# A new prologue and a split last tile in a kernel of windowed attention and a gated feed-forward layer

## Chip, core and metric

The kernel runs on one core of a Trainium2 chip. The metric is the device time of one execution in microseconds (us). Times are medians of several executions, and the profile is one more execution under the hardware profiler; its span is about 1.7 us shorter than the time.

The profile names the engines PE (matmul), PEld (weight load), DVE (vector), ACT (scalar), POOL and SP (which here only issues DMAs).

## The reference

Causal attention over a window of 64 positions, for 8 batches, 8 heads, 576 positions and head size 64, feeds a SwiGLU layer over 4608 tokens (512 to 1536 to 512).

```python
scores = (1/8) * q @ k.T                       # per batch and head
mask = (rel >= 0) & (rel < 64)                 # rel = query position - key position
attn = softmax(where(mask, scores, -1e9))
x = (attn @ v), heads side by side             # 4608 x 512
out = (silu(x @ w_gate) * (x @ w_val)) @ w_out # float32
```

## The kernel before

All engines get their instructions from one list; a helper derives the semaphore waits from what each operation reads and writes. Each engine works through its own part in program order. An operation that waits holds up all that is behind it on its engine.

A tile is 128 tokens. For tile n, `T(n)` transposes q and k, `Sx(n, half)` makes the scores of four heads and the exponential, `AV(n, half)` multiplies by v and normalizes, and `X(n)` transposes the result into xT for the feed-forward part. `F(c, f)` makes one of 12 blocks of the hidden layer (hT) for a chunk of four tiles, and `O(c, u)` the output of one tile. The loaded tiles are kn, qn and va, and T leaves its results in kT and qz. F(0,0) begins with the first matmul on Wg, so "the first Wg matmul" below marks the end of the prologue. The first four tiles have their own prologue, because the first F needs all four.

```python
def first_T(self, pr):                    # one head pair: k and q share a PSUM bank
    tb = bank[:, :].bitcast(BF).rearrange("p (w j t) -> p w j t", w=2, j=4)
    # PE: 8 transposes; then DVE copies k to kT, ACT and DVE copy the halves of q to qz
    g.op("act", ... qz half 0 ..., reads=[bk, (bk, "k")])   # after the k copy
    g.op("dve", ... qz half 1 ..., reads=[bk])

def init_nmask(self):                     # additive mask, made from the 0/1 mask
    self.g.op("dve", lambda e: e.tensor_scalar(self.nmask[:, :], m[:, :], -1.0, 30000.0, ALU.add, ALU.mult), ...)

def load_v(self, n):                      # va: v of tile n.  vb: v shifted by 64 rows, made from va by DMA
    ... pool: va <- v in HBM
    g.op("sp", lambda e: e.dma_start(vb[64:128], va[0:64]), reads=lo, ...)
    g.op("sp", lambda e: e.dma_start(vb2[0:64], va[64:128]), reads=hi, ...)   # vb of tile n + 1

# build(), prologue
self.first_casts(0); self.init_pt(); self.first_T(0); self.first_T(1)
self.first_casts(1); self.init_nmask()
self.Sx(0, 0, True); self.Sx(1, 0, True)
self.first_T(2); self.Sx(2, 0, True)
self.first_T(3); self.Sx(3, 0, True)
for n in range(4):
    self.Sx(n, 1, True); self.AV(n, 0)
for n in range(4):
    self.AV(n, 1)
    if n > 0: self.X(n - 1, "act")
self.X(3, "act")
... # then F(0, 0..5), T(4), F(0, 6), ...

# build(), end: the last chunk's F, with O of the chunk before between them, then
for u in range(4):
    self.O(NFC - 1, u)        # 12 matmuls of 512 columns, one ACT copy, one DMA from SP
```

The softmax here doesn't subtract the row's maximum and nothing guards it: scores larger than these inputs give would overflow.

## Time and profile before

| kernel before | |
|---|---|
| time, median | 376.6 us |
| span of the profile | 375.07 us |
| PE busy | 352.3 us (94%) |
| end of the last xT copy, after which F(0,0) starts | 25.83 us |
| last stretch of idle PE that ends on hT | 361.24 us |

The first lines are from the page: the span, the busy times, the busy tenths of PE in 40 slices and the engines' shares in the chain of waits.

```profile
span 375.1 us, 6635 instructions
PE 352.3 (94%) x2624; PEld 192.0 (51%) x2624; DVE 254.6 (68%) x550; ACT 152.3 (41%) x260; POOL 107.5 (29%) x136
PE   1589999999899999999999999999999999999986
PE 81%; DVE 13%; ACT 3%; DMA 2%; issue 1%
```

PE is full except in the first two or three slices (9.4 us each) and a little at the end. A change of prologue and end can only win what is there. The next lines are PE's timeline in the prologue (start, duration, engine, line, operation; in brackets the idle time before it and what ended it).

```profile
7.68 1.89 PE L302 MATMUL ps<-ident,c 128*128 128x128 bf16 x16 [7.68 <-ACT c L292]
12.69 0.29 PE L388 MATMUL ps<-nmask,ident 128*128 128x128 bf16 x1 [3.12 <-DVE nmask L266]
12.77 0.32 PE L389 MATMUL ps<-qz,kT 128*128 128x128 bf16 x1
12.88 0.32 PE L388 MATMUL ps<-nmask,ident 128*128 128x128 bf16 x1
...
18.65 0.23 PE L388 MATMUL ps<-nmask,ident 128*128 128x128 bf16 x1 [0.72 <-DVE qz L317]
18.71 0.22 PE L389 MATMUL ps<-qz,kT 128*128 128x128 bf16 x1
18.77 0.22 PE L388 MATMUL ps<-nmask,ident 128*128 128x128 bf16 x1
...
21.18 0.19 PE L419 MATMUL ps<-vb,pt 128*128 128x65 bf16 x1
...
25.88 1.04 PE L466 MATMUL ps<-xT,Wg 128*128 128x512 bf16 x4 [0.69 <-ACT xT L450]
```

PE waits 3.12 us for the mask bias (nmask) and later for a copy on DVE (qz). AV(3), at 21.18 us, waits for nothing: the last vb copy that it needs had landed at 19.42. Look at the starts, too: near 12.8 us the matmuls start every 0.107 us, near 18.7 us every 0.056 us. PE's clock has doubled in between. The trace's clock record, which starts with the switch, puts it at 17.73 us.

The end, from the timeline of all engines:

```profile
360.50 0.69 DVE L476 SCALAR_TENSOR_TENSOR hT<-uu,ps 128x512 bf16<-128x512 bf16 x1
361.24 10.54 PE L489 MATMUL ps<-Wo,hT 128*128 128x512 bf16 x48 [1.27 <-DVE hT L476]
...
371.81 0.60 ACT L494 ACTIVATE ost<-ps 128x512 f32<-128x512 f32 x1 [1.99 <-PE ps L489]
372.43 0.33 SPq L496 DMA_DIRECT2D out_dram<-ost  x1
```

PE idles for the elementwise work of the last F, then makes the last four output tiles. Behind the last of them stand an ACT copy of 0.60 us and a DMA of 256 KB.

### The profile page before, as it was taken

The page shows a single profiled execution, that of the slowest core. Times are in us where ns is not written, and L with a number is a line of the kernel's source. Part 1 is how long each engine was busy: PE and PEld are TensorE (multiplying, and loading weights), DVE is VectorE, ACT ScalarE, POOL GpSimd, SP SyncE. Part 2 cuts the span into 40 slices and gives each one's busy share as a digit, 9 for nine tenths or more (in the row PEclk, how much of TensorE's full clock was granted, in tenths as well). Part 3 has the DMA queues.
Part 4 walks back from the last instruction along what each step waited for, and adds up shares of the span by engine and source line. Part 5 has one row for each costly group of instructions (what it writes and reads, how often), then busy time and mean ns, then how long its engine had stood idle before and what let it go on. Part 6 is the DMA issues. An engine that isn't in the chain of part 4 may idle for free.

```text
span 375.1 us, 6635 instructions
## 1 busy us (share of the span) xinstructions
PE 352.3 (94%) x2624; PEld 192.0 (51%) x2624; DVE 254.6 (68%) x550; ACT 152.3 (41%) x260; POOL 107.5 (29%) x136
## 2 busy tenths in 40 slices
PE   1589999999899999999999999999999999999986
PEld 1564555555455555555555555555555555444432
DVE  6668876688867777777777777777777777655520
ACT  2553535435444444444444444444444444233311
POOL 8985525434222222322222222422220000000000
PEclk9999999999999999999999999999999999999999
DMA  9999999979957777777888787877771000010012
GB/s 236 202 201 175 204 173 205 169 47 91 84 71 85 86 86 87 82 88 87 90 87 89 78 94 86 86 83 77 78 82 37 30 29 30 28 58 28 28 38 104
DMA packets 126158, 35.61 MB, mean 95 GB/s; under 512 B 108272, under 2 KB 121520, under 8 KB 126128
## 3 DMA queue, kind: packets, MB, share of 16 engines
q0 software_dynamic: 113152, 17.83, 64.3%
q1 hardware_dynamic: 11920, 16.31, 13.5%
q10 hardware_dynamic: 1056, 1.05, 0.9%
q8 instruction: 21, 0.34, 0.4%
q14 instruction: 9, 0.07, 0.1%
HBM read 37.75 MB, written 9.44 MB: 126 GB/s over the span
## 4 chain that ended last, share of the span: by engine, by line
PE 81%; DVE 13%; ACT 3%; DMA 2%; issue 1%
PE ps L466 41%; PE ps L489 25%; PE ps L389 5%; DVE hT L476 4%; DVE uu L474 4%; PE ps L360 3%; PE ps L441 2%; PE ps L420 2%; PE ps L419 2%; DVE xb L429 2%; DMA f<-in_q_dram 2%; ACT sig L472 1%; DVE pt L407 1%; ACT qz L366 1%; PE ps L302 1%
## 5 line engine op out<-in xcount | busy, mean ns | idle before, releaser
L474 DVE SCALAR_TENSOR_TENSOR uu<-sig,ps 128x512 bf16<-128x512 bf16 x108 | 74.1, 686 | 65.1 <-ACT sig L472 65.1
L466 PE MATMUL ps<-xT,Wg 128*128 128x512 bf16 x432 | 111.0, 380 | 2.4 <-DVE xT L448 1.7
L466 PE MATMUL ps<-xT,Wv 128*128 128x512 bf16 x432 | 110.9, 379 | 0.0
L489 PE MATMUL ps<-Wo,hT 128*128 128x512 bf16 x432 | 98.7, 380 | 2.1 <-DVE hT L476 2.1
L472 ACT ACTIVATE sig<-ps 128x512 bf16<-128x512 f32 x108 | 64.0, 592 | 43.4 <-PE ps L466 43.4
L277 POOL DMA_DIRECT2D qn<-in_q_dram x36 | 30.4, 847 | 164.2 <-PE ps L360 161.3
L476 DVE SCALAR_TENSOR_TENSOR hT<-uu,ps 128x512 bf16<-128x512 bf16 x108 | 74.2, 687 | 3.7
L466 PEld LDWEIGHTS ps<-xT,Wv 128*128 128x128 bf16 x432 | 42.2, 98 | 51.0
L489 PEld LDWEIGHTS ps<-Wo,hT 128*128 128x128 bf16 x432 | 40.9, 98 | 46.9 <-DVE hT L476 2.7
L401 ACT ACTIVATE pt<-ps 128x512 bf16<-128x512 f32 x72 | 42.9, 596 | 33.2 <-PE ps L389 30.5
L466 PEld LDWEIGHTS ps<-xT,Wg 128*128 128x128 bf16 x432 | 38.2, 98 | 32.6 <-DVE xT L448 2.0
L494 ACT ACTIVATE ost<-ps 128x512 f32<-128x512 f32 x36 | 21.5, 597 | 74.8 <-PE ps L489 74.8
L366 ACT ACTIVATE qz<-ps 64x512 bf16<-64x512 bf16 x32 | 18.9, 590 | 57.8 <-DVE kT L365 57.8
L328 POOL DMA_DIRECT2D va<-in_v_dram x40 | 34.7, 875 | 1.3 <-DVE wup L226 0.8
L389 PE MATMUL ps<-qz,kT 128*128 128x128 bf16 x288 | 30.8, 225 | 2.0 <-ACT qz L366 0.4
L429 DVE TENSOR_TENSOR xb<-ps,rc 128x256 bf16<-128x256 f32 x72 | 30.6, 425 | 2.5
L277 POOL DMA_DIRECT2D kn<-in_k_dram x36 | 30.7, 858 | 1.2 <-DMA Wv<-in_moe_w_val_dram 0.8
L448 DVE COPY xT<-ps 128x512 bf16<-128x512 bf16 x32 | 13.6, 423 | 24.1 <-PE ps L441 24.1
L407 DVE TENSOR_TENSOR pt<-pt,mask 128x512 bf16<-128x512 bf16 x64 | 26.6, 416 | 1.5 <-ACT pt L401 1.4
L419 PE MATMUL ps<-vb,pt 128*128 128x65 bf16 x288 | 26.9, 194 | 0.1
L420 PE MATMUL ps<-va,pt 128*128 128x65 bf16 x288 | 27.0, 194 | 0.0
L419 PEld LDWEIGHTS ps<-vb,pt 128*128 128x128 bf16 x288 | 22.6, 98 | 7.3 <-DVE xT L448 0.2
(44 smaller groups left out, 198.6 us busy)
## 6 DMA issues: line engine op xcount, KB each, us to landing
out_dram<-ost SPq DMA_DIRECT2D x36, 256.0 KB, 2.0
vb<-va SPq DMA_DIRECT2D x71, 80.0 KB, 2.1
va<-in_v_dram POOLq DMA_DIRECT2D x32, 128.0 KB, 4.5
qn<-in_q_dram POOLq DMA_DIRECT2D x28, 128.0 KB, 3.4
kn<-in_k_dram POOLq DMA_DIRECT2D x28, 128.0 KB, 4.4
Wo<-in_moe_w_out_dram POOLq DMA_DIRECT2D x2, 768.0 KB, 19.2
Wg<-in_moe_w_gate_dram POOLq DMA_DIRECT2D x5, 256.0 KB, 12.7
Wv<-in_moe_w_val_dram POOLq DMA_DIRECT2D x5, 256.0 KB, 13.3
```

The costliest lines, as they stand in the source:

```text
L277: self.g.op("pool", lambda e, d=d, a=a: e.dma_start(d, a), writes=ks, dma=True)
L328: g.op("pool", lambda e, d=d, a=a: e.dma_start(d, a), writes=ks, dma=True)
L389: r = e.matmul(sv[:, w, c], self.kT[:, pr, k0:k0 + 128], qz[:, pr, :, 64 * w:64 * w + 64], start=not bias, stop=True)
L401: g.op("act", lambda e: e.activation(po, si, ACTF.Exp, scale=SCALE), reads=[bk], writes=[pk])
L419: e.matmul(av[:, j, :], pt[:, h, 0:128], vb[:, h, 0:65], start=True, stop=False)
L420: r = e.matmul(av[:, j, :], pt[:, h, 64:192], va[:, h, 0:65], start=False, stop=True)
L429: g.op("dve", lambda e: e.tensor_tensor(xo, av[:, :, 0:64], rb, ALU.mult), reads=[bk, ("rc", ir)], writes=[("xb", ix, half)])
L466: r = e.matmul(bank[:, :], W[:, kk, f * 128:f * 128 + 128], xT[:, kk, :], start=(kk == 0), stop=(kk == NK - 1))
L472: g.op("act", lambda e: e.activation(sig[:, :], G[:, :], ACTF.Tanh, scale=0.5), reads=[gk], writes=[("sig", i)])
L474: g.op("dve", lambda e: e.scalar_tensor_tensor(uu[:, :], sig[:, :], 1.0, G[:, :], ALU.add, ALU.mult), reads=[("sig", i), gk], writes=[("uu ...
L476: g.op("dve", lambda e: e.scalar_tensor_tensor(hT[:, f, :], uu[:, :], 0.5, V[:, :], ALU.mult, ALU.mult), reads=[("uu", i), vk], writes=[(" ...
L489: r = e.matmul(OB[:, :], hT[:, f, 128 * u:128 * u + 128], self.Wo[:, f, :], start=(f == 0), stop=(f == NF - 1))
```

## The change

The intent is to shorten both ends. In the prologue, k and q are transposed into separate PSUM banks with larger copies, nmask is built on POOL with no detour over mask, and 13 dummy matmuls on zeros run while PE waits for data, to bring up its clock. At the end, O of the tile before goes behind the last F, and the last tile is made as two column halves, copied by two engines and stored from two queues.

```diff
+        g.op("dve", lambda e: e.memset(self.wz[:, :], 0.0), writes=["wz"])
+        g.op("dve", lambda e: e.memset(self.nmask[:, :], 0.0), writes=["nmask"])
-    def init_pool_b(self):          # mask only, then init_nmask on DVE
+    def init_mask(self, m, key, fill):   # the same three POOL operations for nmask and for mask
...
-    def first_T(self, pr):
+    def first_T(self, which, half):      # two head pairs of k, or of q, in one bank
...
+            g.op("dve", lambda e: e.tensor_copy(kd, ks), reads=[bk], writes=kk)   # 128x1024
...
+    def warm(self, count):
+                r = e.matmul(bank[:, :], self.wz[:, 0:128], self.wz[:, :], start=True, stop=True)
...
+    def O_last(self, c, u):              # two halves of 256 columns: ACT + SP queue, DVE + ACT queue
...
-        self.first_casts(0)
+        self.warm(13)
         self.init_pt()
-        (first_T(0), first_T(1), first_casts(1), init_nmask, Sx and first_T(2), first_T(3) interleaved)
+        for half in range(2):
+            self.first_cast("k", half)
+            self.first_cast("q", half)
+        for half in range(2):
+            self.first_T("k", half)
+            self.first_T("q", half)
+        for n in range(4):
+            self.Sx(n, 0, True)
...
+                late = c == NFC - 1 and u == 3
-                if c > 1:
+                if c > 1 and not late:
                     self.O(c - 1, u)
                 self.F(c, 3 * u + 2)
+                if late:
+                    self.O(c - 1, u)
...
-        for u in range(4):
+        for u in range(3):
             self.O(NFC - 1, u)
+        self.O_last(NFC - 1, 3)
```

More of the change, by code (lines that the diff above doesn't have):

```diff
@@ L190, in alloc @@
         self.nmask = sb("nmask", 4 * 64)
+        self.wz = sb("wz", 512)
         self.pt = [t[:, :].rearrange("p (h x) -> p h x", h=H) for t in ring("pt", self.NP, H * 192)]
@@ L251, in init_pool_a @@
             pattern=[[-1, 128]], channel_multiplier=1), writes=["ident"])
-    def init_pool_b(self):
-        m = self.mask
+    def init_mask(self, m, key, fill):
         mm = m[:, :].rearrange("p (a q) -> p a q", a=4)
         self.g.op("pool", lambda e: e.affine_select(
-            out=mm, in_=mm, compare_op=ALU.is_gt, fill=0.0, base=0,
-            pattern=[[0, 4], [-1, 64]], channel_multiplier=1), writes=["mask"])
+            out=mm, in_=mm, compare_op=ALU.is_gt, fill=fill, base=0,
+            pattern=[[0, 4], [-1, 64]], channel_multiplier=1), writes=[key])
         self.g.op("pool", lambda e: e.affine_select(
-            out=mm, in_=mm, compare_op=ALU.is_ge, fill=0.0, base=64,
-            pattern=[[0, 4], [1, 64]], channel_multiplier=-1), writes=["mask"])
-        self.g.op("pool", lambda e: e.memset(m[0:64, 128:192], 0.0), writes=["mask"])
-    def init_nmask(self):
-        m = self.mask
-        self.g.op("dve", lambda e: e.tensor_scalar(self.nmask[:, :], m[:, :], -1.0, 30000.0, ALU.add, ALU.mult),
-                  reads=["mask"], writes=["nmask"])
+            out=mm, in_=mm, compare_op=ALU.is_ge, fill=fill, base=64,
+            pattern=[[0, 4], [1, 64]], channel_multiplier=-1), writes=[key])
+        self.g.op("pool", lambda e: e.memset(m[0:64, 128:192], fill), writes=[key])
     def load_qk(self, n):
@@ L285, in first_loads, with first_cast @@
                 self.g.op(eng, lambda e, d=d, a=a: e.dma_start(d, a), writes=[(nm, half)], dma=True)
-    def first_casts(self, half):
+    def first_cast(self, which, half):
         hs = slice(4 * half, 4 * half + 4)
-        ck = self.ck[:, :, hs].rearrange("p j h d -> p h j d")
-        cq = self.cq[:, :, hs].rearrange("p j h d -> p h j d")
-        self.g.op("dve", lambda e: e.tensor_copy(ck, self.fk[:, hs]), reads=[("fk", half)], writes=[("ck", half)])
-        self.g.op("act", lambda e: e.activation(cq, self.fq[:, hs], ACTF.Copy), reads=[("fq", half)], writes=[("cq", half)])
@@ L294, in first_T @@
-    def first_T(self, pr):
+        dst, src, eng = (self.ck, self.fk, "dve") if which == "k" else (self.cq, self.fq, "act")
+        d = dst[:, :, hs].rearrange("p j h d -> p h j d")
+        rk, wk = [("f" + which, half)], [("c" + which, half)]
+        if eng == "dve":
+            self.g.op("dve", lambda e: e.tensor_copy(d, src[:, hs]), reads=rk, writes=wk)
+        else:
+            self.g.op("act", lambda e: e.activation(d, src[:, hs], ACTF.Copy), reads=rk, writes=wk)
+    def first_T(self, which, half):
@@ L295, in first_T @@
         g = self.g
         bank, bk = self.bank("a")
-        tb = bank[:, :].bitcast(BF).rearrange("p (w j t) -> p w j t", w=2, j=4)
+        tb = bank[:, :].bitcast(BF).rearrange("p (c j t) -> p c j t", c=2, j=4)
+        src = self.ck if which == "k" else self.cq
         def pe(e):
-            for w, src in ((0, self.ck), (1, self.cq)):
+            for c in range(2):
+                pr = 2 * half + c
                 for j in range(4):
-                    r = e.transpose(tb[:, w, j, :], src[:, j, 2 * pr:2 * pr + 2, :], self.ident[:, :])
+                    r = e.transpose(tb[:, c, j, :], src[:, j, 2 * pr:2 * pr + 2, :], self.ident[:, :])
@@ L303, in pe @@
             return r
-        g.op("pe", pe, reads=["ident", ("ck", pr // 2), ("cq", pr // 2)], writes=[bk])
-        kd = self.kT[:, pr, 64:576].rearrange("p (t j) -> p t j", j=4)
-        kk = [("kT", n, pr) for n in range(4)]
-        g.op("dve", lambda e: e.tensor_copy(kd, tb[:, 0].rearrange("p j t -> p t j")), reads=[bk], writes=kk + [(bk, "k")])
+        g.op("pe", pe, reads=["ident", ("c" + which, half)], writes=[bk])
+        prs = slice(2 * half, 2 * half + 2)
+        if which == "k":
+            kd = self.kT[:, prs, 64:576].rearrange("p c (t j) -> p c t j", j=4)
+            ks = tb.rearrange("p c j t -> p c t j")
+            kk = [("kT", n, p) for n in range(4) for p in (2 * half, 2 * half + 1)]
+            g.op("dve", lambda e: e.tensor_copy(kd, ks), reads=[bk], writes=kk)
+            return
@@ L309, in first_T @@
         for e_, eng in ((0, "act"), (1, "dve")):
             ps = slice(64 * e_, 64 * e_ + 64)
-            d = self.qza[ps, :, pr, e_, :].rearrange("p r (t j) -> p r t j", j=4)
-            a = tb[ps, 1].rearrange("p j (r t) -> p r t j", r=4)
-            zk = [("qz", n, pr, e_) for n in range(4)]
-            if eng == "act":
-                g.op("act", lambda e, d=d, a=a: e.activation(d, a, ACTF.Copy), reads=[bk, (bk, "k")], writes=zk)
-            else:
-                g.op("dve", lambda e, d=d, a=a: e.tensor_copy(d, a), reads=[bk], writes=zk)
+            zk = [("qz", n, p, e_) for n in range(4) for p in (2 * half, 2 * half + 1)]
@@ new lines, in ev, with pe @@
+            def ev(e, ps=ps, e_=e_, eng=eng):
+                for c in range(2):
+                    d = self.qza[ps, :, 2 * half + c, e_, :].rearrange("p r (t j) -> p r t j", j=4)
+                    a = tb[ps, c].rearrange("p j (r t) -> p r t j", r=4)
+                    r = e.activation(d, a, ACTF.Copy) if eng == "act" else e.tensor_copy(d, a)
+                return r
+            g.op(eng, ev, reads=[bk], writes=zk)
+    def warm(self, count):
+        bank, bk = self.ps[7], ("ps", 7)
+        def pe(e):
+            for _ in range(count):
+                r = e.matmul(bank[:, :], self.wz[:, 0:128], self.wz[:, :], start=True, stop=True)
+            return r
+        self.g.op("pe", pe, reads=["wz"], writes=[bk])
@@ L496, in O, with pe @@
         g.op("sp", lambda e: e.dma_start(self.out[r0:r0 + 128, :], ost[:, :]), reads=[("ost", io)], dma=True)
+    def O_last(self, c, u):
+        g = self.g
+        ih = c % self.NH
+        hT = self.hT[ih]
+        ost = self.ost[(4 * c + u) % self.NO]
+        io = (4 * c + u) % self.NO
+        r0 = 512 * c + 128 * u
+        for w, eng in ((0, "act"), (1, "dve")):
+            OB, ok = self.bank("o")
+            cs = slice(256 * w, 256 * w + 256)
+            def pe(e, OB=OB, cs=cs):
+                for f in range(NF):
+                    r = e.matmul(OB[:, 0:256], hT[:, f, 128 * u:128 * u + 128], self.Wo[:, f, cs],
+                                 start=(f == 0), stop=(f == NF - 1))
+                return r
+            g.op("pe", pe, reads=[("hT", ih, f) for f in range(NF)] + [("Wo", f) for f in range(NF)], writes=[ok])
+            d, a = ost[:, cs], OB[:, 0:256]
+            if eng == "act":
+                g.op("act", lambda e, d=d, a=a: e.activation(d, a, ACTF.Copy), reads=[ok], writes=[("ost", io), ("osth", w)])
+            else:
+                g.op("dve", lambda e, d=d, a=a: e.tensor_copy(d, a), reads=[ok, ("ost", io)], writes=[("osth", w)])
+            q = "sp" if w == 0 else "act"
+            g.op(q, lambda e, d=d, cs=cs: e.dma_start(self.out[r0:r0 + 128, cs], d), reads=[("osth", w)], dma=True)
     def S(self, n):
@@ L517, in build @@
         self.init_pool_a()
+        self.init_mask(self.nmask, "nmask", -30000.0)
         self.load_v(1)
-        self.init_pool_b()
         self.load_v(2)
@@ L523, in build @@
         W(1, 2)
+        self.init_mask(self.mask, "mask", 0.0)
         for f in range(2, 12, 2):
@@ L527, in build @@
         self.banks("a", [5, 6, 7, 4, 0, 1, 2, 3])
-        self.first_casts(0)
+        self.warm(13)
         self.init_pt()
-        self.first_T(0)
-        self.first_T(1)
-        self.first_casts(1)
-        self.init_nmask()
-        self.Sx(0, 0, True)
-        self.Sx(1, 0, True)
-        self.first_T(2)
-        self.Sx(2, 0, True)
-        self.first_T(3)
-        self.Sx(3, 0, True)
+        for half in range(2):
[6 more added lines that the diff above has]
+            self.Sx(n, 0, True)
         for n in range(4):
```

## The prediction

> **What bounds the kernel now.** The page gives PE 94% of a 375.1 us span, and the chain of waits is PE matmuls for 81%. From 25.9 to 359.8 us PE hardly waits; the change leaves that stretch alone. It acts on the prologue (0 to 25.88 us, the first Wg matmul in the timeline) and on the end.
>
> **Prologue, before (timeline, chain of waits).** The f loads land at 6.1 to 9.8 us; transposes start at 7.68; bias matmuls wait 3.1 us for nmask (12.69); DVE alternates kT and qz copies of 0.69 us, the last ending at 18.6 and releasing the second score half. PE is cold: 128-column matmuls start every 107 ns until 17.7 us, every 56 ns after. The Trainium skill ("TensorE: Matmul & The Clock Gate", Part 1) says that the clock is halved until about 3.4 us of sustained activity; here the switch came 5.0 us after the dense start.
>
> **Prologue, after (estimates from those durations).** Building nmask directly (0.97 us of POOL) removes its wait. 13 dummies of 512 columns, about 0.43 us each cold, run from about 1.3 to 6.8 us and should have PE warm, or nearly, for the scores. But all casts now stand ahead of all copies on DVE, so the second k cast (data at 9.24) holds the first kT copy until about 10.0. Then kT copies of 1.2 us and qz pairs of 1.4 us: first scores near 12.7, second half released near 15.3 instead of 18.65.
>
> Not all of those 3.3 us survive. AV(n) needs the shifted copies vb, whose DMAs follow va. Before, they landed at 15.7 (n=0), 17.0, 18.2 and 19.4 us (n=3). The change does not move that: the DMA row is full, a vb copy takes 5.3 us. AV(3) ran at 21.18 and would now wait until about 19.4. From there to the first Wg matmul took 4.7 us, so F starts near 24.1: 1.8 us gained, with PE gaps beside AV that end on the vb DMA.
>
> It should be kept: T(4), the next PE work that needs late data, ran at 36.25, its kn landed at 33.76 (2.5 us of slack); T(6) had 2.95, AV(4) 3.1. The extra mask ops push POOL's weight issues back about 1 us, but that queue is backlogged by 7 us.
>
> **End.** PE idles from about 359.8 to 361.24 for hT of the last F (DVE 360.50 to 361.19). O(7,3), moved behind the last F (2.6 us of matmul), covers it: 1.4 us. Halving the last tile: 24 matmuls of 256 columns take as long as 12 of 512, the final eviction falls from ACT 0.60 to about 0.4 us on DVE, the final matmul by 0.1, the last DMA is half as large: 0.3 us.
>
> **Sum.** 1.8 + 1.4 + 0.3 = 3.5 us: 376.6 becomes 373.1 us (0.9%), range 371.5 to 374.9. Chances: faster by over 2% 0.03, within 2% 0.95, slower 0.02.
>
> **Signs.** Right: first Wg matmul near 24.1; no DVE hT wait near 360; last O group as 24 short matmuls; nmask gone from the waits; middle as long as before. Wrong: first Wg near 22 means vb is not the limit; near 26, that DVE order or a cold PE ate it; a PE gap at T(4) near 34 us, that the load queue got later.
>
> **What would make it wrong.** PE cooling in the sparse 8 to 19 us, so that the first F runs at half rate (1.5 to 3 us lost); vb landing at another time because POOL's order changed (v(1) issued 1 us later, DVE start 0.4 us later); 256-column pairs paying for weight loads.

## The result

The changed kernel takes 373.29 us (median; 373.20 to 373.52), against 376.61. The ratio is 0.9914 with a 95% interval of 0.9894 to 0.9933: faster by 0.9%. Ratios here are the mean time of one kernel's fast runs over that of the other's in the same rounds, so not quite the ratio of the quoted medians.

The page after:

```profile
span 371.8 us, 6649 instructions
PE 353.7 (95%) x2604; PEld 193.6 (52%) x2649; DVE 254.5 (68%) x550; ACT 151.9 (41%) x260; POOL 108.6 (29%) x139
PE   6779989999899999999999999999999999999997
PE 79%; DVE 12%; DMA 4%; ACT 2%; issue 2%; SPq 1%; POOLq 0%
```

The first two slices of PE are fuller, the first of them with dummies; the third is less full (7 instead of 8 tenths). PE's share of the chain fell and that of DMAs doubled. The prologue on PE:

```profile
1.27 5.09 PE L333 MATMUL ps<-wz 128*128 128x512 bf16 x13 [1.27 <-DVE wz L225]
7.02 1.28 PE L304 MATMUL ps<-ident,c 128*128 128x128 bf16 x16 [0.67 <-DVE c L290]
10.15 0.62 PE L304 MATMUL ps<-ident,c 128*128 128x128 bf16 x8 [1.84 <-DVE c L290]
11.03 0.62 PE L304 MATMUL ps<-ident,c 128*128 128x128 bf16 x8 [0.26 <-ACT c L292]
12.60 0.29 PE L407 MATMUL ps<-nmask,ident 128*128 128x128 bf16 x1 [0.95 <-DVE qz L323]
...
13.00 0.31 PE L407 MATMUL ps<-nmask,ident 128*128 128x128 bf16 x1
13.10 0.31 PE L408 MATMUL ps<-qz,kT 128*128 128x128 bf16 x1
...
18.59 0.19 PE L438 MATMUL ps<-vb,pt 128*128 128x65 bf16 x1 [0.40 <-DMA vb<-va]
...
19.88 0.19 PE L438 MATMUL ps<-vb,pt 128*128 128x65 bf16 x1 [0.45 <-issue]
...
24.80 0.81 PE L485 MATMUL ps<-xT,Wg 128*128 128x512 bf16 x3 [0.92 <-ACT xT L469]
```

The wait for nmask is gone, but the first scores still start at 12.60 us: they now wait for copies on DVE. They run at the slow spacing of 0.107 us in spite of the dummies. AV(2) and AV(3), at 18.59 and 19.88 us, wait for the shifted copies vb. The last line shows three matmuls where four were issued: a record is missing, and the first one really started near 24.58 us, right behind the xT copy that ended at 24.52.

The chain of waits in the same stretch (start, duration, what), first the DMA that released AV(2), then the wait of AV(3), called "issue" by the profile:

```profile
12.92 5.58 DMA vb<-va
...
19.43 0.45 issue
19.88 0.19 PE ps L438
```

What the "issue" hides is seen by asking for the vb copy that AV(3) needs: it was issued at 14.2 us and took 5.6 us, so it landed at 19.79 us, 0.09 us before AV(3) began.

```profile
L351 SPq DMA_DIRECT2D vb<-va x1: 577/577/577, 14.2 to 14.2; - x1
DMA to landing us min/median/max: 5.6/5.6/5.6
```

The clock, in stretches (columns: stretch, length, busy time and count of PE, PEld, DVE, ACT, POOL, granted clock, DMA share, GB/s):

```profile
5.50:12.30 6.80, 3.33 (x36) 2.03 (x34) 4.35 (x8) 3.44 (x5) 6.67 (x11) 1.00 1.79 241
12.30:15.80 3.50, 3.20 (x31) 3.21 (x32) 2.76 (x4) 2.21 (x5) 3.50 (x6) 0.51 1.68 204
15.80:24.50 8.70, 5.97 (x116) 4.93 (x114) 5.14 (x20) 5.31 (x10) 8.70 (x13) 1.00 1.40 219
```

PE became fast at 5.57 us, while the dummies ran, and slow again at 12.39 us, two tenths of a microsecond before the first scores. The end after the change:

```profile
355.93 10.52 PE L508 MATMUL ps<-Wo,hT 128*128 128x512 bf16 x47
...
366.29 2.78 PE L530 MATMUL ps<-Wo,hT 128*128 128x256 bf16 x24
...
369.11 0.42 DVE L539 COPY ost<-ps 128x256 f32<-128x256 f32 x1 [11.81 <-PE ps L530]
369.57 0.36 ACTq L541 DMA_DIRECT2D out_dram<-ost  x1
```

There is no wait for hT any more: O runs through from 355.93 us. The split of the gain at the end of the last xT copy (25.83 and 24.52 us) gives 1.31 us to the prologue. From there to the end of the span takes 349.24 us before and 347.26 after: 1.98 us for the end. The two add up to the 3.3 us between the spans.

### The profile page after: what moved, and what is told of

Its sections match the earlier page's. It is cut to its first block, busy times and chain, and to the rows that moved or that the text cites. A ratio compares the mean times of both kernels' runs of the same rounds, so it can differ in the third digit from the quotient of the medians.

```text
span 371.8 us, 6649 instructions
## 1 busy us (share of the span) xinstructions
PE 353.7 (95%) x2604; PEld 193.6 (52%) x2649; DVE 254.5 (68%) x550; ACT 151.9 (41%) x260; POOL 108.6 (29%) x139
## 3 DMA queue, kind: packets, MB, share of 16 engines
q1 hardware_dynamic: 11920, 16.18, 13.5%
## 4 chain that ended last, share of the span: by engine, by line
PE 79%; DVE 12%; DMA 4%; ACT 2%; issue 2%; SPq 1%; POOLq 0%
PE ps L485 41%; PE ps L508 24%; PE ps L408 5%; DVE uu L493 4%; DVE hT L495 3%; PE ps L379 3%; DMA va<-in_v_dram 2%; PE ps L460 2%; PE ps L438 2%; PE ps L439 2%; DVE xb L448 2%; DMA vb<-va 2%; ACT sig L491 1%; DVE pt L426 1%; ACT qz L385 1%
## 5 line engine op out<-in xcount | busy, mean ns | idle before, releaser
L485 PE MATMUL ps<-xT,Wg 128*128 128x512 bf16 x408 | 105.7, 379 | 3.8 <-DVE xT L467 1.7
L508 PE MATMUL ps<-Wo,hT 128*128 128x512 bf16 x401 | 93.2, 379 | 2.0 <-DVE rc L445 1.0
L508 PEld LDWEIGHTS ps<-Wo,hT 128*128 128x128 bf16 x420 | 39.8, 98 | 43.9 <-DVE hT L495 1.0
```

Of the source, the lines that this page charges most:

```text
L485: r = e.matmul(bank[:, :], W[:, kk, f * 128:f * 128 + 128], xT[:, kk, :], start=(kk == 0), stop=(kk == NK - 1))
L508: r = e.matmul(OB[:, :], hT[:, f, 128 * u:128 * u + 128], self.Wo[:, f, :], start=(f == 0), stop=(f == NF - 1))
```

## The experiments

Each kernel ran with five rounds (one for the last) beside the kernel before, in three series. The kernel before had medians of 376.66, 376.73 and 376.65 us in them. The changed kernel was not run again in these series, so a difference from it is one between series.

### 1. The prologue alone

Edit to the changed kernel:

```diff
-                late = c == NFC - 1 and u == 3
+                late = False
-        for u in range(3):
+        for u in range(4):
             self.O(NFC - 1, u)
-        self.O_last(NFC - 1, 3)
```

> The changed kernel with the old end (O(7,3) before the last F, last tile whole). Additive theory, from the two traces: the first Wg matmul moved from 25.9 to 24.6 us, so the prologue alone is worth 1.3 us: 375.3 us, with the 1.3 us PE wait for hT back near 360. Rival: the prologue's 3 us earlier scores are also felt later (the loads land earlier, fewer waits in the middle), or are lost again at the next late load: then this lies at 374.5 or below, or at 376.5.

It took 375.33 us (ratio 0.9967, 0.9954 to 0.9981). The wait for hT is back in PE's timeline:

```profile
359.77 1.47 PE L508 MATMUL ps<-Wo,hT 128*128 128x512 bf16 x6 [1.27 <-DVE hT L495]
```

The prologue is worth 1.3 us, and the gain of the two ends adds up. The rivals fall.

### 2. The last tile whole

```diff
-        for u in range(3):
+        for u in range(4):
             self.O(NFC - 1, u)
-        self.O_last(NFC - 1, 3)
```

> The changed kernel with the last tile whole again; O(7,3) stays behind the last F. The prediction gave the halves 0.3 us (eviction 0.2, matmul 0.1): then 373.6 us. The traces say 0.6 us (from the last eviction's end to the end of the span 2.69 us before, 2.27 after, so the final DMA saves 0.4 more): then 373.9 us.

It took 373.89 us (ratio 0.9925, 0.9913 to 0.9938), 0.6 us more than the changed kernel. The traces allow a sharper reading, free of what happened in the prologue: from the last xT copy to the end of the span it took 347.63 us, against 347.26. So the halves are worth 0.4 to 0.6 us, more than the 0.3 predicted, and moving O the rest of the 1.98 us, about 1.4 to 1.6.

This profiled run (span 371.5) was shorter than that of the changed kernel (371.8), although the kernel is slower. Its vb landed at 19.15 us instead of 19.79.

### 3. No dummies

```diff
-        self.warm(13)
```

> The changed kernel without the 13 dummy matmuls. Theory: the dummies are worth nothing here, since the first scores run at 107 ns spacing (cold) even with them and AV waits for the vb DMAs: 373.3 us, within 0.3, first Wg matmul at 24.6. Rival: the dummies keep transposes and scores fast and are worth about 1 us: 374.3 us or more, first Wg matmul at 25.6 or later.

It took 373.26 us (ratio 0.9911, 0.9897 to 0.9924): the changed kernel's ratio was 0.9914. The dummies are worth nothing here. The clock rose at 16.27 us, against 15.81 for the final rise with dummies, and AV(3) still waited for vb:

```profile
19.65 0.19 PE L438 MATMUL ps<-vb,pt 128*128 128x65 bf16 x1 [0.42 <-DMA vb<-va]
```

(The mean clock that a run lists is no guide here. The records begin with the first switch to the full clock, so a run without dummies lists 1.00.)

### 4. AV without the wait for vb (wrong result)

```diff
+        fake = n < 4
+        vb = va if fake else vb
...
-    reads=[..., ("va", iv, 1), ("vb", iv, 0), ("vb", iv, 1)]
+    reads=[..., ("va", iv, 1)] + ([] if fake else [("vb", iv, 0), ("vb", iv, 1)])
```

> Wrong result on purpose: in the first four tiles AV reads va in place of the shifted copy vb, so it does not wait for the vb DMAs (which are still made). Theory (vb is what the prologue ends on): AV(3) starts near 18.4 instead of 19.9 us, first Wg matmul near 23.1, total 371.9 us. Rival (DVE and ACT copies, or the cold PE, bound the prologue): first Wg matmul stays near 24.6, total 373.3 us. If the load of kn for T(4) took over, a PE gap of over 0.3 us shows before T(4) near 33.5.

It took 372.09 us (ratio 0.9881, 0.9868 to 0.9895), with a wrong result, as intended. The first Wg matmul moved from 24.58 to 22.86 us, and the next late load came to light at once, before T(4):

```profile
22.86 1.04 PE L487 MATMUL ps<-xT,Wg 128*128 128x512 bf16 x4 [0.69 <-ACT xT L471]
33.86 0.40 PE L379 MATMUL ps<-ident,kn 128*128 128x128 bf16 x4 [0.46 <-DMA kn<-in_k_dram]
```

So vb was what the prologue of the changed kernel ended on. Behind it stands the load of kn, which landed at 33.81 us and gave back half a microsecond.

### 5 and 6. AV tile by tile, and copies earlier: two failures

If only the last tile's work stood behind the last vb, the first F could start earlier. The first try put all scores first:

```diff
         for n in range(4):
             self.Sx(n, 1, True)
-            self.AV(n, 0)
         for n in range(4):
-            self.AV(n, 1)
+            self.AV(n, 0)
             if n > 0:
                 self.X(n - 1, "act")
+            self.AV(n, 1)
```

> The changed kernel with the first four tiles' AV in the order AV(0,0) AV(0,1) AV(1,0) AV(1,1) and so on, all second-half scores ahead of them, so that only the last tile's work (about 2.8 us instead of 4.8) stands behind the last vb landing. Theory (vb landing plus what follows it sets the first Wg matmul): it starts near 22.5 instead of 24.4 us; then T(4), 10.4 us later, must wait 0.3 to 1 us for kn (lands 33.1 to 33.9), so 371.8 us in total instead of 373.3, not 371.4. Rival: ACT's and DVE's work bounds that stretch; then the order changes nothing, 373.3 us.

It took 374.00 us (ratio 0.9941, 0.9912 to 0.9969), 0.7 us slower than the changed kernel. My order was at fault. AV(0) now stood behind all 64 score and bias matmuls, most of them at the slow clock (until 17.99 us), so DVE had nothing to do until 19.15 us. And each X(n-1) stood on PE between the two halves of AV(n), so that tiles could not overlap:

```profile
20.39 0.40 PE L460 MATMUL ps<-ident,xb 128*128 128x128 bf16 x4 [0.80 <-DVE xb L448]
21.77 0.40 PE L460 MATMUL ps<-ident,xb 128*128 128x128 bf16 x4 [0.49 <-DVE xb L448]
23.15 0.40 PE L460 MATMUL ps<-ident,xb 128*128 128x128 bf16 x4 [0.49 <-DVE xb L448]
24.53 0.40 PE L460 MATMUL ps<-ident,xb 128*128 128x128 bf16 x4 [0.74 <-DVE xb L448]
```

Each tile takes 1.38 us on the way from PE to DVE and back. This kernel also scattered: 373.34 and 373.54 us in the two runs with a granted clock of 0.995, 374.0 to 374.5 at 0.990 and 0.991, and 377.67 at 0.982. In the changed kernel, runs at 0.991 (373.25, 373.20) and at 0.995 (373.52, 373.34) do not show it: those at 0.991 were, if anything, faster. (In the profiles of kernels with dummies 0.995 goes with one stretch of 3.41 us at half clock and 0.990 or 0.991 with 6.83 us; by the same sum 0.982 would be about 13.5 us, an estimate.) That fits a clock that costs time only where the scores stand ahead of everything else, but no experiment fixed the clock.

The sixth kernel is the fifth, with the first half's transposes and copies ahead of the second half's casts:

```diff
         for half in range(2):
             self.first_cast("k", half)
             self.first_cast("q", half)
-        for half in range(2):
             self.first_T("k", half)
             self.first_T("q", half)
```

> e5_by_tile, and the first half's transposes and copies put ahead of the second half's casts in program order, so that DVE does not idle 2.4 us for the second k load. Theory: scores start near 10.5 instead of 12.6 us and are all done before vb lands, so nothing is gained over e5_by_tile: same time within 0.2 us. Rival: the copies' chain still matters, 0.5 us or more faster than e5_by_tile.

It took 373.96 us (ratio 0.9931, 0.9919 to 0.9943), the same as the fifth by median. The scores did not start near 10.5 us as expected but at 12.72: in program order they stand behind the second half's transposes. Those waited for the second k cast, which now stood behind the first half's copies on DVE and ended at 10.99 us, and then ran at the slow clock until the scores began. The test said little, then, since my edit did not do what it was for.

### 7. The kernel before, with only nmask built directly and the new end

```diff
+        g.op("dve", lambda e: e.memset(self.nmask[:, :], 0.0), writes=["nmask"])
...
+        self.init_mask(self.nmask, "nmask", -30000.0)
...
-        self.init_nmask()
# and the changed kernel's end; old first_T, no dummies
```

> The kernel before with the new end and with nmask built directly, nothing else: old transposes, no dummies, old order on DVE. Theory: removing the nmask wait starts the first scores at about 11.65 instead of 12.69 and all that follows 1.0 us earlier: last qz copy ends at 17.6, AV(3) near 20.1, only 0.3 to 0.4 us behind the vb landing. So nearly the whole gain of the prologue: 373.7 us against 373.3 of the changed kernel. Rival (the separate banks and dummies carry the gain): 374.3 us or more.

It took 373.81 us (ratio 0.9920, 0.9907 to 0.9933). Kernel 8, in the same rounds, took 373.17. So this one part of the new prologue, with the new end, comes within about 0.6 us of the whole change. Its profiled run, the fastest of the four, is no clean example: the clock rose there at 14.40 us, against 17.73 in the profile of the kernel before.

### 8. The changed kernel, with nmask made on DVE again

```diff
-        self.init_mask(self.nmask, "nmask", -30000.0)
...
+        self.init_nmask()          # from mask, ahead of the casts
         for half in range(2):
             self.first_cast("k", half)
```

> The changed kernel with nmask made from mask on DVE again (0.4 us, ahead of the casts); the rest of the change stays. Theory: the copies end 0 to 0.4 us later, still ahead of vb: 373.3 us, within 0.2. Rival: 373.7 us or more.

It took 373.17 us (ratio 0.9908, 0.9894 to 0.9923), as fast as the changed kernel. Kernels 7 and 8 together: by the medians the direct nmask alone gives 0.7 to 0.8 of the prologue's 1.3 us, and once the separate banks and the new order are there it gives nothing. That fits one limit, the vb landing, that caps both.

### What the profiles say together

In eight profiles AV and X have the order of the changed kernel and AV depends on vb. Times in us, "landing" for the last vb copy that AV(3) needs:

| kernel | landing | last xT copy ends | between |
|---|---|---|---|
| before | 19.42 | 25.83 | 6.41 |
| changed | 19.79 | 24.52 | 4.74 |
| prologue alone | 19.74 | 24.47 | 4.73 |
| last tile whole | 19.15 | 23.88 | 4.73 |
| no dummies | 19.56 | 24.29 | 4.73 |
| nmask on DVE | 19.42 | 24.16 | 4.73 |
| halves on SP (12) | 19.68 | 24.41 | 4.74 |
| nmask and end (7) | 19.44 | 24.39 | 4.95 |

Whatever else differs, the six kernels with the new prologue end it 4.73 or 4.74 us after the landing. Kernel 7 is 0.2 us short of that limit in its profiled run (373.36 us, the fastest of its four), and the kernel before 1.7 us. In the fourth kernel, which does not wait for vb, the rule breaks (19.34 and 22.81).

The landing itself was left where it is. In the changed kernel va of tile 3 had landed at 12.84 us, but the vb copy made from it was issued only at 14.21 us, behind six other copies on SP that took 0.53 to 0.60 us each to issue. No run tried to issue it sooner.

### 9 to 11. The order mended

The ninth kernel is the changed one with AV, scores and X interleaved:

```diff
-        (Sx(n, 1), AV(n, 0) for four tiles; then AV(n, 1) with X(n - 1))
+        self.Sx(0, 1, True); self.AV(0, 0)
+        self.Sx(1, 1, True); self.AV(1, 0); self.AV(0, 1)
+        self.Sx(2, 1, True); self.AV(2, 0); self.AV(1, 1); self.X(0, "act")
+        self.Sx(3, 1, True); self.AV(2, 1); self.AV(3, 0); self.X(1, "act")
+        self.AV(3, 1); self.X(2, "act"); self.X(3, "act")
```

> Corrects the order of e5_by_tile, where all scores stood ahead of AV and each X stood between the two halves of the next AV. Here scores, AV(n,0), AV(n-1,1) and X(n-2) are interleaved, so that DVE works while vb lands and only AV(3,0), AV(3,1) and the last transposes stand behind the last vb. Theory: first Wg matmul near 23.0 (now 24.4), like e4_no_vb_wait but with the right result; T(4) then waits 0 to 0.6 us for kn; total 372.1 us, 1.2 under the changed kernel. Rival (an engine's work, not the vb landing with what is queued behind it, bounds the stretch): 373.0 us or more.

It took 372.10 us with the right result (ratio 0.9880, 0.9865 to 0.9895), 1.2 us less than the changed kernel and the fastest kernel that is correct. Here are the start of AV(3), the last transposes, the first F and T(4):

```profile
20.30 0.19 PE L438 MATMUL ps<-vb,pt 128*128 128x65 bf16 x1
...
22.29 0.40 PE L460 MATMUL ps<-ident,xb 128*128 128x128 bf16 x4 [0.70 <-DVE xb L448]
23.61 0.81 PE L485 MATMUL ps<-xT,Wg 128*128 128x512 bf16 x3 [0.92 <-ACT xT L469]
...
33.75 0.39 PE L379 MATMUL ps<-ident,kn 128*128 128x128 bf16 x4
```

The last xT copy ends at 23.33 us, 3.67 us after vb's landing (19.66) instead of 4.74. But AV(3) started 0.64 us after that landing and did not wait for it: before it PE was busy with scores, at the slow clock until 17.24 us, and behind it the chain of waits runs through DVE. So in this profile vb is no longer what the prologue ends on. The first Wg matmul came near 23.4 us (one of four records is missing again), later than the 23.0 expected. T(4) started 0.19 us after its kn had landed (33.56), without a wait in this run, so there is little room left before that load becomes the limit.

The tenth kernel moves T(4) one F later:

```diff
-        for f in range(6):
+        for f in range(7):
             self.F(0, f)
         self.T(4)
-        self.F(0, 6)
-        self.Sx(4, 0)
         self.F(0, 7)
+        self.Sx(4, 0)
         self.Sx(4, 1)
```

> e9_av_pipelined, and T(4) one F later (after F(0,6)), with both score halves of tile 4 behind F(0,7). If T(4)'s wait for kn takes part of the gain in e9_av_pipelined, this gives it back: 371.7 us and no gap before T(4). If not, the same as e9_av_pipelined, 372.1 us.

It took 372.35 us (ratio 0.9886, 0.9872 to 0.9901), no gain over the ninth. There was no wait for kn to take away, and the new order made one of its own:

```profile
41.02 0.38 PE L408 MATMUL ps<-qz,kT 128*128 128x128 bf16 x4 [0.53 <-ACT qz L385]
```

The eleventh is the tenth without the line `self.warm(13)`.

> e10_av_pipelined_later_T4 without the dummy matmuls. Theory: vb still sets the pace, and the clock has fallen back before the first scores anyway, so they remain worth nothing: within 0.3 us of e10_av_pipelined_later_T4. Rival: with the order improved, the dummies count: slower by 0.5 us or more.

It took 372.42 us (ratio 0.9887, 0.9870 to 0.9903): again the dummies change nothing that these runs can tell. That vb still sets the pace, as the theory had it, the profile does not bear out: AV(3) started at 20.11 us, 0.46 us after its last vb copy had landed.

### 12. Both halves of the last tile from SP

```diff
-            q = "sp" if w == 0 else "act"
+            q = "sp"
```

> The changed kernel with both halves of the last tile stored from the SP queue. In the trace, issue to landing of the last half should be 1.67 us (as the first half from SP has now) instead of 1.74 from ACT, and 2.0 for a whole tile: then size, not the queue, shortens it. The stretch from the last landing to the end of the span was 0.66 us with SP last and 0.43 to 0.49 with ACT last: if the queue is the reason it is 0.65 here, and the kernel 0.1 to 0.2 us slower than the changed one.

It took 373.51 us (two runs; ratio 0.9917). The last half landed 1.70 us after its issue (1.74 from ACT in the changed kernel, 1.98 for a whole tile). So the size shortens the DMA, not the queue. From the landing to the end of the span it took 0.59 us, against 0.48 with ACT and 0.65 for the whole tile. A tenth of a microsecond may belong to the queue; one profile is too little to say so.

## Why the prediction was right

The total was right: 373.1 predicted, 373.29 measured. Point by point:

- **"AV(3) ran at 21.18 and would now wait until about 19.4 ... 1.8 us gained."** The mechanism was right. Earlier scores are cut short by the vb landing (experiment 4 and the table). The size was off: vb landed at 19.79 us instead of 19.4 in the profiled run, and the gain was 1.31 us. The landing moves between the profiles (19.15 to 19.79), and the end of the prologue moves with it.
- **"first scores near 12.7, second half released near 15.3."** They started at 12.60, and the last copy on DVE ended at 15.11. DVE's queue did hold the first kT copy for the second k cast. This cost nothing visible behind vb.
- **"13 dummies ... should have PE warm, or nearly, for the scores."** This failed. The dummies did raise the clock, at 5.57 us (2.7 to 5.7 us after the first dummy in the ten profiles that have them), but it fell again at 12.39, just ahead of the scores, which ran at 0.107 us spacing until 15.8 us. In all ten profiles with dummies the clock fell between 9.7 and 12.4 us. The total did not depend on it, as experiments 3 and 11 show.
- **"It should be kept: T(4) ... 2.5 us of slack."** Right: kn landed at 33.20 and T(4) started at 34.95 us. Pushing POOL's issues back did not make it later. Experiment 4 shows what happens when the slack is used up.
- **"O(7,3), moved behind the last F, covers it: 1.4 us."** Right; kernels 1 and 2 put it at 1.4 to 1.6.
- **"Halving the last tile: ... 0.3 us."** Under-sized: 0.4 to 0.6. The copy shrank by 0.18 us as predicted, the final DMA by 0.24 (1.98 to 1.74), and the rest after the landing by 0.17. The matmul's 0.1 did not appear: O(8,0) to the last copy took 10.57 us before and 10.59 after. The prologue gave 0.5 us less than predicted and the end 0.3 us more, so that the total came within 0.2 us is partly luck.

The Trainium skill carried the argument in two places. "Trainium Kernel Development and Optimization" (Key Constraints) says that DMAs from the SP, ACT and POOL queues share 16 engines and interleave. The trace fits that: beside the weight loads the 80 KB vb copy that AV(3) needs took 5.3 to 5.6 us, against a median of 2.1 over the whole run; no run here took the weight loads away. "TensorE: Matmul & The Clock Gate" (Part 1) gives a free-running window of about 3.4 us for the clock. The traces agree: all stretches between switches that the traces hold in the prologue are 3.41 or 6.83 us long.

## What to carry to other kernels

Before you shorten a stage, list the landing times of everything it will need next: the gain ends at the first of them that does not move. Two parts of a change that attack the same limit do not add up, so undo them one at a time, and do each alone. When the limit is a landing, work on the order behind it: here, letting DVE work while the copies landed gave 1.2 us, nearly as much as the whole new prologue.

## What the Trainium skill lacked or had wrong

- "TensorE: Matmul & The Clock Gate", "Why this matters for your kernels", advises against idle gaps of over about 3 us between bursts of matmuls. Here PE's gaps between the dummies and the scores were 0.67, 1.84, 0.26 and 0.95 us, with 32 transposes among them, and the clock still fell at 12.39 us. Part 4 of the page says that transposes do not count as busy in the same way, which would fit, but the advice on gaps does not mention it. No run here separates transposes from sparse work in general. The page knows other ways to lose the clock, so the point is about that one piece of advice.
- The same page (Part 1) gives about 4 us of sustained work until the clock rises, give or take 0.5 us between runs. The changed kernel's dummies needed 4.3 us, but the ten profiles with dummies spread from 2.7 to 5.7 us. With dense scores from 12.54 us on, in kernel 5, it rose only at 17.99 us, 5.5 us later, and in the kernel before 5.0 us after their start.
- "DMA: Bandwidth & Descriptors", "Anatomy of one DMA", gives about 2.0 us plus 1 us per 436 KB for the POOL path. It has no such fit for the SP path. For stores from SP the slope is close (256 KB in 1.98 us, 128 KB in 1.70: 0.28 us for 128 KB, where the page's figure makes 0.30), but the fixed part is then only about 1.4 us, an estimate from these two sizes. In a busy stretch neither figure serves: a copy of 80 KB from SP took 5.3 to 5.6 us here.
